# Starting three 64 KB-per-partition load buffers at a multiple of 256 bytes in SBUF, in a decode kernel that streams its KV cache

## The chip, the cores and the metric

The kernel runs on one core of a Trainium2 chip. The metric is the device time of one execution in microseconds (us).

The profile is a record of one execution. PE is the matmul engine, DVE is VectorE, ACT is ScalarE, POOL is GpSimd, SP is the engine that issues the transfers. The trace also holds a record of each DMA packet: start, duration, bytes, queue.

## The reference, cut to what matters

```python
B, Sq, D = 2, 1, 1024
H, Sk, Dh = 32, 16384, 128
# k_cache, v_cache: (B, H, Sk, Dh) bf16, 268 MB each
q = (x @ wq).reshape(B, Sq, H, Dh).transpose(0, 2, 1, 3)
scores = einsum("bhqd,bhkd->bhqk", q, k_cache) * Dh ** -0.5
o = einsum("bhqk,bhkd->bhqd", softmax(scores), v_cache)
a = o.transpose(0, 2, 1, 3).reshape(B, Sq, H * Dh) @ wo
b = ...   # layer norm, two small linear layers, an MLP 1024 -> 3584 -> 1024
out = g * a + (1 - g) * b          # g = sigmoid(sum(x * gate_w))
```

One query per head against 16,384 keys: each byte of the caches is read once and hardly used. With the weights that is 572.5 MB from HBM.

## The kernel before

Everything large passes through a ring of three buffers of 65,536 bytes a partition, which make up 192 KB of each partition of SBUF. A transfer of K or of V fills one buffer whole (128 partitions x 65,536 bytes, 8.39 MB). The pools are laid out in the order in which they are entered, so the buffers start where the small constants end:

```python
    const = ctx.enter_context(tc.tile_pool(name="const", bufs=1))
    big = ctx.enter_context(tc.tile_pool(name="big", bufs=NBIG))       # NBIG = 3
    tpool = ctx.enter_context(tc.tile_pool(name="tpool", bufs=2))
    # ... (cut)
    def big_tile(name):
        return big.tile([P, SLOT], BF16, tag="big", name=name)         # SLOT = 32768 elements

    def load_k(i):
        t = big_tile("Kn")
        nc.sync.dma_start(
            out=t[:].rearrange("p (j d) -> p j d", d=Dh), in_=cache_rows(A_k_cache, i)
        )
```

`cache_rows` gives each partition one run of 65,536 bytes of HBM, and its place in the buffer is one run too. Per K buffer, DVE makes 16 transposes into the tile T and PE 64 matmuls on S; per V buffer, PE makes 64 matmuls on O. A transfer is issued when the buffer three transfers back has been used up.

As built, the constants end at byte 20,640 of the partition. The three buffers start at 20,640, 86,176 and 151,712: each is 160 bytes past a multiple of 256.

Of the kernel before, what the change touches and what calls it, by code (L numbers as in the profile page):

```python
# [10 lines left out]
FP32 = mybir.dt.float32  # L11
BF16 = mybir.dt.bfloat16
# [11 lines left out]
def kernel(  # L24
# [16 lines left out]
    P = nc.NUM_PARTITIONS  # L41
# [4 lines left out]
    G = 2  # L46
# [10 lines left out]
    SLOT = NJ * Dh  # L57
    NBIG = 3

    const = ctx.enter_context(tc.tile_pool(name="const", bufs=1))  # L60
    big = ctx.enter_context(tc.tile_pool(name="big", bufs=NBIG))
    tpool = ctx.enter_context(tc.tile_pool(name="tpool", bufs=2))
    ppool = ctx.enter_context(tc.tile_pool(name="ppool", bufs=1))
    stat = ctx.enter_context(tc.tile_pool(name="stat", bufs=2))
# [86 lines left out]
        out=perm[:].rearrange("k (h a) -> k h a", a=4),  # L151
        in_=ident_f[:].rearrange("k (a h) -> k h a", a=4),
    )
    neg_half = const.tile([P, 1], FP32)
    nc.vector.memset(neg_half[:], -0.5)
    ones_f = const.tile([P, P], FP32)
    nc.vector.memset(ones_f[:], 1.0)

    hmask = const.tile([P, G], FP32)
    nc.vector.memset(hmask[:], 0.0)  # L160
    for a in range(G):
        nc.vector.memset(hmask[64 * a : 64 * a + 64, a : a + 1], 1.0)



    kill = const.tile([P, 1], FP32)
    kill4 = const.tile([P, 4], FP32)
    for a in range(4):
        c0 = 32 * a + (16 if a < 2 else 0)
# [22 lines left out]
            channel_multiplier=1,  # L192
        )

    own = const.tile([P, 8], BF16)
    nc.vector.memset(own[:], 0.0)
    for a in range(4):
        nc.vector.memset(own[32 * a : 32 * a + 32, 2 * a : 2 * a + 2], 1.0)
# [411 lines left out]
```

## Time and profile before

Time before: 1341.06 us, the median of three runs (1341.02 to 1341.31). The page of the kernel before, its span, its engines' busy shares and its two busiest DMA queues (packets, MB, share of 16 engines' time):

```profile
span 1339.3 us, 12650 instructions
PE 830.6 (62%) x5415; PEld 380.9 (28%) x5415; DVE 709.3 (53%) x863; ACT 45.6 (3%) x100; POOL 14.5 (1%) x45
...
q1 hardware_dynamic: 12664, 572.54, 99.1%
q8 instruction: 42, 0.69, 0.2%
```

No compute engine is near full, and the 16 DMA engines together are at work 99.1% of the span. The windows view says the same by stretch; its last columns are the granted matmul clock, the DMA share and GB/s:

```profile
20.00:400.00 380.00, 246.34 (x1698) 115.62 (x1699) 215.66 (x265) 12.08 (x28) 4.76 (x12) 0.83 1.00 431
400.00:800.00 400.00, 251.35 (x1603) 118.22 (x1602) 213.52 (x253) 13.89 (x31) 3.37 (x10) 0.79 1.00 432
800.00:1200.00 400.00, 251.68 (x1435) 109.36 (x1434) 228.56 (x259) 13.65 (x30) 3.38 (x10) 0.81 1.00 432
```

The list of DMA issues gives the median time from issue to landing. A K or V transfer moves 8.39 MB, which at 432 GB/s takes 19.4 us; 37.7 us to land means that it was issued while nearly a whole other transfer was still ahead of it. So the DMA engines never wait for an issue:

```profile
Kn<-in_A_k_cache_dram SPq DMA_DIRECT2D x32, 52.3
Vn<-in_A_v_cache_dram SPq DMA_DIRECT2D x31, 37.7
```

The main compute groups (busy us and mean ns | idle before):

```profile
L307 PE MATMUL S<-T,z 128*128 128x512 bf16 x2048 | 596.2, 424 | 326.2 <-DVE T L299 310.3
L299 DVE STREAM_TRANSPOSE T<-Kn 128x1024 f32<-128x1024 f32 x512 | 612.0, 1229 | 267.5 <-DMA Kn<-in_A_k_cache_dram 218.6
```

And two moments of the timeline (start us, length): the last matmuls on O, which waited for the last V transfer, and the cast of the result:

```profile
1298.44 3.63 PE L351 MATMUL O<-Vn,PT 128*32 128x512 bf16 x32 [4.90 <-DMA Vn<-in_A_v_cache_dram]
...
1336.04 0.42 DVE L575 CAST rows<-out_acc 128x256 bf16<-128x256 f32 x1 [31.21 <-PE out_acc L392]
```

The packet records, gathered by size (this is a count over the trace's records, not a view of the profile):

```
kernel before, main queue; ns
bytes     packets  minimum  median   mean
4096        256      159      159    161.0
8192        768      309      313    314.3
14336       512      535      538    539.9
57344       128     2116     2119   2129.1
65536      8192     2418     2420   2426.0     (1431 of 8192 at 2418; 68 over by more than 100 ns)
```

From 4096 to 65,536 bytes the minimum rises by 2259 ns for 61,440 bytes: 27.2 GB/s for one engine, 435 GB/s for sixteen. With 8.4 ns a packet on top, that gives the minima at both ends.

### The profile page before, as it was taken

The page shows a single profiled execution, that of the slowest core. Times are in us where ns is not written, and L with a number is a line of the kernel's source. Part 1 is how long each engine was busy: PE and PEld are TensorE (multiplying, and loading weights), DVE is VectorE, ACT ScalarE, POOL GpSimd, SP SyncE. Part 2 cuts the span into 40 slices and gives each one's busy share as a digit, 9 for nine tenths or more (in the row PEclk, how much of TensorE's full clock was granted, in tenths as well). Part 3 has the DMA queues.
Part 4 walks back from the last instruction along what each step waited for, and adds up shares of the span by engine and source line. Part 5 has one row for each costly group of instructions (what it writes and reads, how often), then busy time and mean ns, then how long its engine had stood idle before and what let it go on. Part 6 is the DMA issues. An engine that isn't in the chain of part 4 may idle for free.

```text
span 1339.3 us, 12650 instructions
## 1 busy us (share of the span) xinstructions
PE 830.6 (62%) x5415; PEld 380.9 (28%) x5415; DVE 709.3 (53%) x863; ACT 45.6 (3%) x100; POOL 14.5 (1%) x45
## 2 busy tenths in 40 slices
PE   2577655677657755555776555577655556765664
PEld 2233222433225322222332222233222223322231
DVE  0666565366651665545666544556655455665530
ACT  0000000000000000000000000000000000000000
POOL 0000000000000000000000000000000000000000
PEclk9988877688776877778887777888777788877775
DMA  9999999999999999999999999999999999999997
GB/s 408 435 437 434 435 423 437 424 439 433 433 431 430 436 436 433 427 429 427 437 437 435 433 433 424 435 435 431 435 431 433 435 437 425 435 427 429 434 422 291
DMA packets 12728, 573.34 MB, mean 428 GB/s; under 512 B 1784, under 2 KB 1792, under 8 KB 2560
## 3 DMA queue, kind: packets, MB, share of 16 engines
q1 hardware_dynamic: 12664, 572.54, 99.1%
q8 instruction: 42, 0.69, 0.2%
q14 instruction: 14, 0.11, 0.0%
q10 hardware_dynamic: 8, 0.00, 0.0%
HBM read 572.53 MB, written 0.00 MB: 427 GB/s over the span
## 4 chain that ended last, share of the span: by engine, by line
PE 27%; DVE 24%; DMA 19%; another core or an unknown queue 14%; issue 13%; ACT 3%; SPq 0%; ACTq 0%; POOL 0%
DVE T L299 20%; PE S L307 14%; DMA Kn<-in_A_k_cache_dram 13%; PE O L351 7%; DMA Vn<-in_A_v_cache_dram 3%; DMA wo<-in_A_wo_dram 3%; PE misc L212 2%; PE misc L361 2%; PE misc L486 2%; ACT Pr L335 1%; DVE PT L339 1%; ACT Os L359 1%; DVE mx L328 1%; DVE mdiag L321 1%
## 5 line engine op out<-in xcount | busy, mean ns | idle before, releaser
L307 PE MATMUL S<-T,z 128*128 128x512 bf16 x2048 | 596.2, 424 | 326.2 <-DVE T L299 310.3
L299 DVE STREAM_TRANSPOSE T<-Kn 128x1024 f32<-128x1024 f32 x512 | 612.0, 1229 | 267.5 <-DMA Kn<-in_A_k_cache_dram 218.6
L307 PEld LDWEIGHTS <-z 128*128 128x128 bf16 x2048 | 218.4, 107 | 698.3 <-issue 535.7
L351 PE MATMUL O<-Vn,PT 128*32 128x512 bf16 x2048 | 121.4, 390 | 4.9 <-DMA Vn<-in_A_v_cache_dram 4.9
L378 DVE SCALAR_TENSOR_TENSOR OT<-misc,g_bc,rinv 128x2 bf16<-128x2 f32 x32 | 7.0, 219 | 158.3 <-PE misc L361 158.3
L351 PEld LDWEIGHTS <-PT 128*32 128x32 bf16 x2048 | 74.1, 140 | 51.0 <-issue 22.0
L212 PE MATMUL misc<-rs,ones_f 128*128 128x2 f32 x64 | 17.8, 348 | 79.1 <-DVE rs L371 79.1
L359 ACT COPY Os<-O 128x512 f32<-128x512 f32 x32 | 18.8, 586 | 1070.2 <-PE O L351 1070.2
L361 PE MATMUL misc<-osel,Os 128*128 128x2 f32 x256 | 33.7, 254 | 22.2 <-ACT Os L359 22.2
L318 DVE TENSOR_REDUCE m<-S 128x1 f32<-128x512 f32 x32 | 22.1, 692 | 36.9 <-PE S L307 36.9
L361 PEld LDWEIGHTS misc<-osel,Os 128*128 128x128 f32 x256 | 31.0, 191 | 37.1 <-ACT Os L359 37.1
L212 PEld LDWEIGHTS misc<-rs,ones_f 128*128 128x128 f32 x64 | 16.0, 310 | 83.9 <-issue 81.2
L339 DVE STREAM_TRANSPOSE PT<-Pr 128x512 bf16<-128x512 bf16 x32 | 22.7, 711 | 28.7 <-ACT Pr L335 28.7
L335 ACT ACTIVATE Pr<-S,nb 128x512 bf16<-128x512 f32 x32 | 22.0, 687 | 125.3 <-DVE nb L330 122.3
L212 PE MATMUL misc<-mdiag,ones_f 128*128 128x128 f32 x64 | 15.6, 326 | 16.9 <-DVE mdiag L321 16.9
L486 PEld LDWEIGHTS <-wt 128*128 128x128 bf16 x352 | 22.3, 172 | 9.8 <-DMA wt<-in_B_w_dram 8.5
L328 DVE TENSOR_REDUCE mx<-misc 64x1 f32<-64x64 f32 x64 | 14.2, 222 | 18.9 <-PE misc L212 18.5
L275 POOL TENSOR_TENSOR z<-qsel,own 128x32 bf16<-128x32 bf16 x32 | 10.8, 337 | 1208.6 <-PE S L307 1177.3
L250 PE MATMUL misc<-xT,wt 128*128 128x2 bf16 x256 | 7.1, 165 | 23.3 <-DVE xT L245 20.7
L486 PE MATMUL misc<-xn2T,wt 128*128 128x2 bf16 x224 | 14.4, 202 | 8.3 <-DMA wt<-in_B_w_dram 8.3
L375 DVE RECIPROCAL rinv<-misc 128x2 f32<-128x2 f32 x32 | 5.5, 170 | 22.6 <-PE misc L212 22.6
L575 DVE CAST rows<-out_acc 128x256 bf16<-128x256 f32 x1 | 0.4, 424 | 31.2 <-PE out_acc L392 31.2
(78 smaller groups left out, 98.8 us busy)
## 6 DMA issues: line engine op xcount, KB each, us to landing
Vn<-in_A_v_cache_dram SPq DMA_DIRECT2D x2, 4096.0 KB, 47.1
wt<-in_B_w_dram SPq DMA_DIRECT2D x1, 7168.0 KB
w<-in_B_w_dram SPq DMA_DIRECT2D x4, 1792.0 KB, 33.0
wo<-in_A_wo_dram SPq DMA_DIRECT2D x6, 1024.0 KB, 34.7
wt<-in_B_w_dram SPq DMA_DIRECT2D x2, 2048.0 KB, 37.2
wo<-in_A_wo_dram SPq DMA_DIRECT2D x2, 512.0 KB, 18.9
wo<-in_A_wo_dram SPq DMA_DIRECT2D x4, 256.0 KB, 12.8
Kn<-in_A_k_cache_dram SPq DMA_DIRECT2D x32, 52.3
```

The costliest lines, as they stand in the source:

```text
L212: nc.tensor.matmul(ps[:], lhsT=ones_f[:], rhs=src, start=True, stop=True)
L299: nc.vector.transpose(out=T[:].rearrange("p w j s -> p j w s"), in_=Kw[:, m * CW : (m + 1) * CW].rearrange("p (j w e) -> p j w e", w=2, e=32),
L307: nc.tensor.matmul(S[:], lhsT=z[:, v, NM - 1 - m : NM - 1 - m + P], rhs=Tb[:, v // 2, :, v % 2], start=(m == 0 and v == 0), stop=(m == NM ...
L318: nc.vector.reduce_max(out=m[:], in_=S[:], axis=AX.X)
L321: nc.vector.tensor_scalar(out=mdiag[:], in0=ident_f[:], scalar1=m[:, 0:1], scalar2=None, op0=ALU.mult)
L328: nc.vector.reduce_max(out=mx[pa, :], in_=mall[pa, pa], axis=AX.X)
L335: nc.scalar.activation(out=Pr[:], in_=S[:], func=ACTF.Exp, bias=nb[:], scale=scale, accum_out=rs[:])
L339: nc.vector.transpose(out=PT[:], in_=Pr[:])
L351: nc.tensor.matmul(O[32 * g : 32 * g + 32, :], lhsT=PT[:, m : CJ * 32 : 16], rhs=V[:, j0 : j0 + 4, :], start=(m == 0), stop=(m == NM - 1),)
L359: nc.scalar.copy(out=Os[:].rearrange("p x d -> p (x d)"), in_=O[:])
L361: nc.tensor.matmul(oc[:], lhsT=Os[:, x, :], rhs=osel[:, x, :], start=(x == 0), stop=(x == 3))
L486: nc.tensor.matmul(ps[:, c, :], lhsT=w[:, r, :].rearrange("k (p c) -> k p c", c=C)[:, :, c], rhs=actT[:, r, :], start=(r == 0), stop=(r == ...
```

## The change

The intent is to start each buffer at a multiple of 256 bytes. The pool of buffers moves to the front. Only 256 bytes lie between byte 16,384, where the tiles begin as built, and the buffers: the language's own four constants (128 bytes) and four small tiles of this kernel (32 bytes each as allocated).

```diff
+    small = ctx.enter_context(tc.tile_pool(name="small", bufs=1))
+    big = ctx.enter_context(tc.tile_pool(name="big", bufs=NBIG))
     const = ctx.enter_context(tc.tile_pool(name="const", bufs=1))
-    big = ctx.enter_context(tc.tile_pool(name="big", bufs=NBIG))
@@
-    neg_half = const.tile([P, 1], FP32)
+    neg_half = small.tile([P, 1], FP32)
@@
-    hmask = const.tile([P, G], FP32)
+    hmask = small.tile([P, G], FP32)
@@
-    kill = const.tile([P, 1], FP32)
+    kill = small.tile([P, 1], FP32)
@@
-    own = const.tile([P, 8], BF16)
+    own = small.tile([P, 8], BF16)
```

As built, the buffers start at 16,640, 82,176 and 147,712, all multiples of 256. The tiles behind (T, Pr, PT, statistics) keep their addresses. The instructions and their order are the same on all five engines.

## The prediction

> **What bounds the kernel now.** The transfers. The page's queue list gives the main DMA queue 99.1% of the time of 16 engines; the windows view shows a DMA share of 1.00 and 431 to 432 GB/s from 20 to 1280 us. The matmul engine is 62% busy, VectorE 53%. The chain of waits names transposes and matmuls, but these only hand buffers back: a V load lands 37.7 us after its issue, about two transfers, so another one is always running and the DMA engines never run dry.
>
> By the trace's packets: 8192 of them carry 65,536 bytes each, minimum 2418 ns, median 2420, mean 2426. Minima of 159 ns at 4096 bytes and 2418 at 65,536 give 27.2 GB/s for one engine plus a constant of 8.4 ns a packet. Sixteen of these make 435.2 GB/s[...]. So: 572.5 MB at that slope 1315.6 us; about 680 data packets per engine x 8.4 ns 5.7 us; time over the minima 6 us; 1.8 us before the first packet; the rest is the tail.
>
> **What the change does.** Order and number of instructions stay the same on all engines; only addresses move. As built, the three buffers start 160 bytes past a multiple of 256 before, and at one after. T, Pr, PT and the statistics keep their addresses; constants swap places with the buffers, costed at nothing.
>
> [...] The whole constant would be 5.7 us. [...]
>
> Against it: [...] The 4-byte semaphore packets take 9 ns, and the first small loads' 16-byte packets 9 ns too[...]. So the constant may have nothing to do with alignment, and the gain be 0. [...]
>
> **Predicted.** 1338.8 us (before 1341.06), 8 in 10 between 1335.8 and 1341.8: in truth two places, near 1337 and near 1341. Faster by over 2%: 0.01; within 2%: 0.98; slower by over 2%: 0.01.
>
> **What would show it.** Right, if the minimum of the 65,536-byte packets falls from 2418 to about 2412 ns, and that of the 4096-byte ones from 159 to 153: the same nanoseconds at every size. Wrong, if the minima stay. Transposes (1229 ns) and matmuls on S (424 ns) should keep their means, apart from the clock. The tail after the last V transfer, from about 1298 us, should shrink by tenths at most.
>
> **What would make it wrong.** [...]

The sum: about 6 ns less in each of about 680 packets an engine came to 4.0 us, so near 1337, at somewhat less than an even chance, against a gain of 0, near 1341. The forecast of 1338.8 us, 2.3 under 1341.06, lies between these two. The trace has the 8.4 ns a packet (from the minima of 159 and 2418 ns); that 6 of them hang on the alignment was not shown. Cut with it are the reason given why a gain over 2% has no room, a doubt whether a write pays at all for its alignment, and a risk: if the time over the minima comes from misaligned writes that meet the engines' reads, aligned ones could save up to 4 us more, or lose as much.

## The result, and the profile after

The changed kernel takes 1337.38 us (median of 4 runs, 1337.28 to 1337.59), the kernel before 1341.18 us beside it (4 runs, 1341.02 to 1341.39): 3.8 us less. The ratio is 0.9972 with a 95% interval of 0.9954 to 0.9989. It is the mean time of one kernel's fast runs over that of the other's of the same rounds, so not quite the ratio of the medians.

The lines of the page after (line numbers are one higher than before):

```profile
span 1335.5 us, 12650 instructions
PE 830.0 (62%) x5415; PEld 381.4 (29%) x5415; DVE 709.2 (53%) x863; ACT 45.5 (3%) x100; POOL 14.3 (1%) x45
...
q1 hardware_dynamic: 12664, 572.54, 99.2%
```

The windows view after: the same DMA share, 1 GB/s more in each stretch.

```profile
20.00:400.00 380.00, 245.95 (x1702) 115.63 (x1703) 216.40 (x266) 12.07 (x28) 4.71 (x12) 0.83 1.00 432
400.00:800.00 400.00, 251.01 (x1605) 118.17 (x1604) 213.95 (x253) 13.88 (x31) 3.32 (x10) 0.79 1.00 433
800.00:1200.00 400.00, 253.82 (x1439) 109.99 (x1437) 228.87 (x259) 13.63 (x30) 3.31 (x10) 0.81 1.00 433
```

The issues and the compute groups after. Transfers land a little sooner; transposes and matmuls take what they took, so nothing came from the compute engines:

```profile
Kn<-in_A_k_cache_dram SPq DMA_DIRECT2D x32, 51.9
Vn<-in_A_v_cache_dram SPq DMA_DIRECT2D x31, 37.4
```

```profile
L308 PE MATMUL S<-T,z 128*128 128x512 bf16 x2048 | 594.0, 423 | 324.7 <-DVE T L300 309.7
L300 DVE STREAM_TRANSPOSE T<-Kn 128x1024 f32<-128x1024 f32 x512 | 611.8, 1229 | 264.1 <-DMA Kn<-in_A_k_cache_dram 215.8
```

The two moments of the timeline after:

```profile
1295.12 3.64 PE L352 MATMUL O<-Vn,PT 128*32 128x512 bf16 x32 [5.05 <-DMA Vn<-in_A_v_cache_dram]
...
1332.26 0.42 DVE L576 CAST rows<-out_acc 128x256 bf16<-128x256 f32 x1 [29.92 <-PE out_acc L393]
```

The last V data is used 3.3 us earlier (1298.44 to 1295.12) and the result is cast 3.8 us earlier (1336.04 to 1332.26). The gain was gathered evenly along the stream, and 0.5 us of it in the weight pieces at the end.

Even the packet records look alike at first, in the minimum and in the transfer rate. The difference is in how many packets reach the minimum:

```
65,536-byte packets       before    after
minimum, ns                 2418     2418   (one packet of after: 2415)
median, ns                  2420     2418
mean, ns                  2426.0   2422.8
at 2418 or less            17.5%    96.9%
over by 1 to 99 ns          6693      182
over by 100 ns and more       68       76
4096-byte packets: 159 at best in both; at 159: 161 of 256 before, 256 of 256 after
```

Below, "short excess" is the mean time over 2418 ns of the long packets, without those over by 100 ns and more. It is 3.38 ns before and 0.29 ns after. By transfer, in the order in which they ran, it goes like this (ns, the first 14 of the 64 transfers with such packets, and the last three):

```
before  1.0 6.3 1.9 1.2 2.2 1.8 2.7 2.6 3.4 3.4 3.9 3.4 3.3 3.2 ... 3.3 3.4 3.5
after   1.5 8.6 1.2 2.0 0.2 0.8 0.5 2.5 0.4 0.0 0.7 0.2 0.0 0.0 ... 0.0 0.0 0.0
```

Both begin alike. Then the kernel before settles at 3.5 ns and the kernel after at nothing.

The sum, in means over 16 engines: from the first data packet to the end of the last takes 1333.3 us before and 1329.7 after, 3.6 us less. Long packets give 1.7 us of that (1242.12 to 1240.46), shorter data packets 0.6 (84.20 to 83.60), instruction fetches on the other queues 0.4 (3.24 to 2.88), idle engines 1.0 (2.9 to 1.9, nearly all in the last 16 us). These are rounded and overlap a little at the edges. About half of the idle part has a visible source: the engines finish their shares of the last 14,336-byte pieces 3.0 us apart before (1312.05 to 1315.09) and 2.4 us apart after (1309.30 to 1311.66), so that the mean engine is done 2.1 us ahead of the slowest before and 1.6 us after.

### The profile page after: what moved, and what is told of

It reads as the page before. It is cut to its first block, busy times and chain, and to the rows that moved or that the text cites. A ratio compares the mean times of both kernels' runs of the same rounds, so it can differ in the third digit from the quotient of the medians.

```text
span 1335.5 us, 12650 instructions
## 1 busy us (share of the span) xinstructions
PE 830.0 (62%) x5415; PEld 381.4 (29%) x5415; DVE 709.2 (53%) x863; ACT 45.5 (3%) x100; POOL 14.3 (1%) x45
## 4 chain that ended last, share of the span: by engine, by line
PE 27%; DVE 24%; DMA 19%; another core or an unknown queue 14%; issue 13%; ACT 3%; SPq 0%; ACTq 0%; POOL 0%
DVE T L300 20%; PE S L308 14%; DMA Kn<-in_A_k_cache_dram 13%; PE O L352 7%; DMA Vn<-in_A_v_cache_dram 3%; DMA wo<-in_A_wo_dram 3%; PE misc L213 2%; PE misc L362 2%; PE misc L487 2%; ACT Pr L336 1%; DVE PT L340 1%; ACT Os L360 1%; DVE mx L329 1%; DVE mdiag L322 1%
## 5 line engine op out<-in xcount | busy, mean ns | idle before, releaser
L300 DVE STREAM_TRANSPOSE T<-Kn 128x1024 f32<-128x1024 f32 x512 | 611.8, 1229 | 264.1 <-DMA Kn<-in_A_k_cache_dram 215.8
```

The lines of the kernel that those rows point to most:

```text
L300: nc.vector.transpose(out=T[:].rearrange("p w j s -> p j w s"), in_=Kw[:, m * CW : (m + 1) * CW].rearrange("p (j w e) -> p j w e", w=2, e=32),
```

## The experiments

Twelve kernels were run. All keep T within 96 bytes of its old address, and T stays exactly in place in all but the last. Each is compared with the kernel before on the same chip. All passed the comparison with the reference, also those that compute a wrong attention: the comparison does not notice it (probably because the attention adds very little to the output; this was not looked into).

A column used in the tables is the pace: the mean time from one 8.39 MB transfer to the next, taken from the mean start of their packets, over the 50 such steps after the first dozen that have no weight load between them. It is 19.426 us before and 19.386 after. Times 68 (572.5 MB are 68 such transfers) the difference of 0.039 us makes 2.7 of the 3.8 us. A step between mean starts covers the second half of one transfer and the first half of the next; this matters in experiment 6.

### 1. Offset, or place of the constants?

The change does two things: it moves the start of the buffers to a multiple of 256, and it moves most constants, which all engines read, from in front of the buffers to behind them. Two kernels do one each. `off160` keeps the new order and pushes the buffers back to 160:

```diff
-    g_bc = const.tile([P, B], FP32)
-    omg_bc = const.tile([P, B], FP32)
+    g_bc = small.tile([P, B], FP32)
+    omg_bc = small.tile([P, B], FP32)
@@ the same for xn1T, hT, shT (32 bytes each)
```

> Pools in the order of the changed kernel (small constants, big buffers, other constants), but five 32-byte constants more in front, so that the buffers start 160 bytes past a multiple of 256, as in the kernel before; T keeps its address. Theory A (what counts is the offset of the buffers): 1341 us, and about 80% of the 65,536-byte packets over the minimum of 2418 ns again, by 3.5 ns on the mean. Theory B (what counts is that most constants, which all engines read, moved away from in front of the buffers): 1337.4 us, and over 95% of the long packets at 2418 ns.

`first0` keeps the old order and takes 160 bytes of constants away from in front:

```diff
     big = ctx.enter_context(tc.tile_pool(name="big", bufs=NBIG))
+    late = ctx.enter_context(tc.tile_pool(name="late", bufs=1))
@@
-    g_bc = const.tile([P, B], FP32)
+    g_bc = late.tile([P, B], FP32)
@@ the same for omg_bc, xn1T, hT, shT
```

> Pools in the order of the kernel before (constants in front of the buffers), but five 32-byte constants put behind them, so that the buffers start at a multiple of 256 (here also of 4096); T keeps its address. Theory A (offset): 1337.4 us, over 95% of the long packets at the minimum of 2418 ns. Theory B (place of the constants): 1341 us, 80% of them above it.

Measured:

```
kernel   offset mod 256   constants   us (median, 5 runs)   at 2418 ns   short excess   pace us
off160        160          behind          1341.15            18.0%        3.45 ns      19.426
first0          0          in front        1337.39            97.3%        0.21 ns      19.387
the kernel before beside them: 1341.16 us (9 runs)
```

Theory A, the offset, holds on both sides; the place of the constants is worth nothing. `first0` also lies at a multiple of 4096, and is no faster for it.

### 2. Which multiple?

The same edit with one, two or four tiles moved gives offsets of 32, 64 and 128.

> As the changed kernel, with two 32-byte constants more in front: buffers 64 bytes past a multiple of 256. Theory A1 (a write must start at a multiple of 256[...]): about 1341 us, most long packets above 2418 ns, by 3 to 4 ns on the mean. Theory A2 (only whole 64-byte units matter; 160 is a multiple of 32 but not of 64): 1337.4 us, over 95% of the packets at 2418 ns.

> As the changed kernel, with four 32-byte constants more in front: buffers 128 bytes past a multiple of 256. A1 (256): about 1341 us. A2 (64) or a unit of 128: 1337.4 us. A cost that grows with the offset up to half of 256 would show 128 as dear as or dearer than 160 and 64 at about half.

> As the changed kernel, with one 32-byte constant more in front: buffers 32 bytes past a multiple of 256, the least offset that the pools allow. All or nothing, as 64, 128 and 160 showed: 1341.2 us, 70 to 90% of the long packets above 2418 ns. If 32 bytes cost less than the others: between 1337.4 and 1341.

```
offset mod 256   us (median)   kernel before beside it   at 2418 ns   short excess   pace us
   0  (after)      1337.38            1341.18              96.9%        0.29 ns      19.386
  32               1342.08            1341.34               5.0%        4.49 ns      19.436
  64               1341.36            1341.16              11.5%        3.67 ns      19.428
 128               1341.19            1341.16              27.4%        3.47 ns      19.427
 160 (before)      1341.18              -                  17.5%        3.38 ns      19.426
```

Multiples of 64 and of 128 bring nothing (A2 falls). Of the offsets tried only 0 is free. The cost is not in proportion to the offset: 64, 128 and 160 cost 3.8 to 4.0 us over the changed kernel. The expectation "all or nothing" missed for 32, which costs 4.7 us over the changed kernel (4.5 if each is set against the kernel before on its own chip): it is 0.74 us over the kernel before on its chip (the others at most 0.2), with 95% of its packets over 2418 ns instead of the expected 70 to 90%. Offsets of 96, 192 and 224 were not tried.

### 3. Do the writes meet the engines' reads?

The prediction's own suspect was that misaligned writes meet the compute engines' reads of SBUF. `light160` and `light0` do a sixteenth of the work on each K and V buffer, at the old and at the new offset; the transfers are all there. Their outputs are wrong, which doesn't matter for the times.

```diff
-        for m in range(NM):          # transposes and matmuls on S
+        for m in range(1):
@@
-        for m in range(NM):          # matmuls on O
+        for m in range(1):
@@ start and stop flags to match
```

> Wrong result on purpose. The kernel before (buffers at 160) with a sixteenth of the work on each K and V buffer: one transpose of 16 and four matmuls of 64 on S, four of 64 on O; all transfers stay. Theory C (the time over the minimum comes from writes that meet the engines' reads and writes of SBUF): the mean short excess of the long packets falls from 3.5 ns to under 0.5 ns, and the time to about 1337 us. Theory D (it comes from the transfers among themselves): the excess stays at 3 to 4 ns and the time at about 1341 us less at most 1 us of the tail.

> Wrong result on purpose. The changed kernel with the same sixteenth of the work. C and D alike: about 1337 us, nearly all long packets at 2418 ns; it is the partner of the run before. If both light kernels take the same time, C holds; if they are 3 to 4 us apart, D.

The span, and the group of transposes, of the light kernel with offset 160:

```profile
span 1332.8 us, 4072 instructions
...
L299 DVE STREAM_TRANSPOSE T<-Kn 128x1024 f32<-128x1024 f32 x32 | 39.8, 1245 | 353.3 <-DMA Kn<-in_A_k_cache_dram 353.3
```

and of the light kernel with offset 0:

```profile
span 1329.6 us, 4072 instructions
...
L300 DVE STREAM_TRANSPOSE T<-Kn 128x1024 f32<-128x1024 f32 x32 | 39.8, 1245 | 352.0 <-DMA Kn<-in_A_k_cache_dram 352.0
```

512 transposes have become 32 and 612 us of them 39.8, and still the two kernels are 3.2 us apart: 1334.56 and 1331.39 us (5 runs each). At offset 160 the short excess is 3.48 ns, as with full work (3.38); at offset 0 it is 0.10. Theory C falls, D holds in the main: the excess in the packets is as large with a sixteenth of the compute. The totals are 6.7 us (offset 160) and 6.0 us (offset 0) lower than with full work, which D had not foreseen (it allowed 1 us). The 6.0 us are there without any misalignment, so they aren't the effect under study; the last section comes back to them. The other 0.6 us is the difference between 3.8 and 3.2 us; whether compute adds that much to the cost of the offset was not tested.

### 4. Source or destination?

The offset could count where a transfer reads, where it writes, or as a shift between the two. These two kernels read K and V from 160 bytes further on in HBM, once with the destination at 160 (same shift on both sides) and once at 0. The values are then wrong.

```diff
-        return cache[b, hg * G : (hg + 1) * G].rearrange("a s d -> (a s) d").rearrange(
-            "(p j) d -> p j d", p=P
-        )
+        e0 = (b * H + hg * G) * Sk * Dh + (80 if i < NT - 1 else 0)
+        return cache.rearrange("b h s d -> (b h s d)")[e0 : e0 + P * SLOT].rearrange(
+            "(p j d) -> p j d", p=P, d=Dh
+        )
```

> Wrong result on purpose. The kernel before (buffers at 160), and every K and V transfer but the last pair reads its 65,536 bytes a partition from 160 bytes further on in HBM, so that source and destination have the same offset to a multiple of 256. Theory R (what costs is the shift between source and destination): 1337.4 us, most long packets at 2418 ns. Theory W (what costs is where the write starts): 1341 us as before, excess 3.5 ns. [...]

> Wrong result on purpose. The changed kernel (buffers at a multiple of 256), reading K and V from 160 bytes further on in HBM. Theory R (shift between source and destination): 1341 us, excess 3.5 ns. Theory W (where the write starts): 1337.4 us, over 95% of the long packets at 2418 ns. [...]

```
kernel           source shifted by   destination mod 256   us (median)   at 2418 ns   short excess
src160_dst160          160                  160              1341.27        16.7%       3.39 ns
src160_dst0            160                    0              1337.45        97.3%       0.21 ns
the kernel before beside them: 1341.25 us
```

Theory W holds: where the write starts is what counts. Shifting the read by 160 bytes changes nothing, neither the minimum (2418 ns with the shift and without, but for single packets of 2415) nor the excess. (That the caches themselves start at a multiple of 256 in HBM is assumed; no run shows their addresses.)

### 5. One engine alone, or only in company?

`alone160` and `alone0` append eight loads of K rows into one buffer after the end of the kernel, each waiting for the one before, so that they meet neither compute nor other loads. (The scheduler put the first of them before the output, where it met the last weights. The second of each pair is read.)

```diff
+    pt = big_tile("probe")
+    for n in (17, 17, 34, 34, 68, 68, 128, 128):
+        nc.sync.dma_start(
+            out=pt[0:n, :].rearrange("p (j d) -> p j d", d=Dh), in_=cache_rows(A_k_cache, 0)[0:n]
+        )
```

> The kernel before with eight more loads into one buffer (at 160) after the end, each waiting for the one before it: 17, 17, 34, 34, 68, 68, 128, 128 partitions of 65,536 bytes, of which the second of each pair counts. If a DMA uses as many engines (up to 16) as divide its partitions, these run on 1, 2, 4 and 16 engines, and the engine count can be read from how many packets run at once. Theory D1 (engines get in each other's way[...]): alone, on 1 engine, every packet takes 2418 ns; the excess comes with 16. Theory D2[...]: an excess of 3 to 4 ns on the mean on 1 engine too.

> The changed kernel with the same eight loads (buffer at a multiple of 256), as partner. D1 and D2: 2418 ns for nearly every packet at every engine count, but for the first packets of a load, which start together.

(D1: the excess comes only with company. D2: each engine pays for its misaligned writes by itself.)

How many engines ran is read as the sum of the packets' times over the load's length; it comes near the 1, 2, 4 and 16 that the expectation supposed:

```
partitions  engines   short excess at offset 160   at offset 0    GB/s (160 / 0)
   17         1.0              0.00 ns               1.50 ns       26.4 / 26.5
   34         2.0              0.00                  0.75          53.1 / 52.8
   68         3.8       (see the last section)                     69.3 / 69.9
  128        15.5              1.23                  1.57         407.8 / 410.1
```

On one engine, at the costly offset, every packet but the first takes 2418 ns exactly. So an engine that runs by itself pays nothing for a misaligned write, in loads of 17 packets: D2 falls as far as these short loads go. But D1's second half was not met either: 16 engines in one isolated load show no more excess at 160 than at 0. The cost appeared only where all engines streamed for longer. That agrees with the series by transfer above, where both kernels begin alike and part after some five to ten transfers, that is 40 to 80 packets an engine. One engine alone was not tried for so long, so company and duration are not told apart here; experiment 6 speaks for company. `alone0` is not at 2418 ns for nearly every packet, as expected, but at 2420 for many; I have no reason for these 2 ns.

### 6. Does each buffer pay for itself?

Two theories: by P each packet pays for the offset of its own buffer, in the company of others; by L one misaligned buffer spoils all. Here the three buffers lie at 0, 32 and 64 past a multiple of 256:

```diff
-        return big.tile([P, SLOT], BF16, tag="big", name=name)
+        return big.tile([P, SLOT + 16], BF16, tag="big", name=name)[:, 0:SLOT]
```

> The changed kernel with 32 bytes between the buffers: the first starts at a multiple of 256, the second 32 bytes and the third 64 bytes past one (T moves by 96 bytes). Theory P[...]: a third of the long packets at 2418 ns, mean short excess a third of 0 + 4.6 + 3.8, so 2.8 ns; time 1337.4 + (0 + 4.7 + 4.0)/3 = 1340.3 us. Theory L[...]: under 25% of the packets at 2418 ns, excess 3.5 ns or more, 1341 us or more.

Measured: 1340.39 us (5 runs), beside 1341.21 for the kernel before; 56.8% of the long packets at 2418 ns, short excess 2.03 ns.

```
buffer, in the order of use            0        64        32
step to the next transfer, us        19.385   19.435    19.419
the same steps, changed kernel       19.377   19.398    19.383
more than there, us                   0.008    0.037     0.036
short excess, ns                      0.9       0.8       4.4
short excess, all three there, ns     0.01      3.77      4.63
(all after the first dozen transfers)
```

The time is the one that theory P gave (1340.3), but the bill by buffer is not P's. A step holds half of a transfer and half of the next, so each difference is half the sum of what its two transfers cost, and the three have to be solved for the buffers: my estimate from them is about 0.01 us a transfer for the buffer at 0, 0.01 for the one at 64 and 0.065 for the one at 32. P had nothing, 0.042 and 0.050 (the paces of experiment 2 over the changed kernel's). The packets say the same: the buffer at 64 is nearly free here, and the one at 32 pays in full. P's packets missed too (56.8% at the minimum, not a third). That its total came out is a coincidence of sizes. Theory L falls by its numbers (under 25% at the minimum, 1341 us or more).

The records show one thing more. After the first dozen transfers, 236 packets into the aligned buffer overlap in time (by more than 20 ns) with a packet that another engine writes into the buffer at 32: their short excess is 3.1 ns on the mean, against 0.6 ns for the 1799 that do not. For the buffer at 64 it is 2.8 ns (265 packets) against 0.5 (2024). In the changed kernel such packets at the edge of a transfer are not late (0.01 ns over all its later packets). So packets come late beside other engines' writes into the buffer at 32, also when their own buffer is aligned. Why the buffer at 64 costs 3.77 ns a packet when all three lie there and so little here is not known.

## Why the prediction was right or wrong

The time was right: 1338.8 predicted, 1337.38 measured, within the range of 1335.8 to 1341.8, and near the first of its "two places, near 1337 and near 1341". What bounds the kernel was right: with the same compute (1229 ns a transpose before and after) the time fell by what the transfers gained. The slope of 27.2 GB/s did not move (minima of 159 and 2418 ns in both kernels), and the gain was 0.28%, far from 2%; that the slope could not move was not shown.

The step that failed is the one that carried the number: about 6 of the 8.4 ns a packet as a cost of the alignment, 4.0 us in all. The prediction gave its own test, the minimum "falls from 2418 to about 2412 ns, and that of the 4096-byte ones from 159 to 153", and "Wrong, if the minima stay." They stayed at 2418 and 159. The 8.4 ns a packet are no cost of this misalignment; one engine alone at offset 160 also takes 2418 ns a packet. Nor does the cost grow with the offset: 32 cost more than 160 (1342.08 against 1341.18 us).

What happened stood in the prediction's last paragraph as a risk: the time over the minima (2426 against 2418) shrank, for which up to 4 us were allowed. That term, put at zero in the sum, is where the gain is: the share of long packets above the minimum went from 83% to 3%. But the reason given there, writes that meet the engines' reads, is wrong as well, for at least 3.2 of the 3.8 us: so far apart the two offsets still were with a sixteenth of the compute. And the mean excess that vanished is 3 ns, not the 8 between 2426 and 2418: more than half of those 8 are some 70 packets over by 100 ns and more, which stayed. That two wrong causes gave the right size is luck: the 4.0 us of the one happen to be near the 3.8 us measured.

The doubt whether a write pays at all had the wrong end: a shifted read costs nothing here (1341.27 against 1341.25 us), and the write is what counts (1337.45 us with its start at a multiple of 256). "The tail ... should shrink by tenths at most" was right: 0.5 of the 3.8 us came after the last V data was used.

What is shown: the offset of the destination to a multiple of 256 is the cause; the place of the constants and the source's offset are not, nor, for the most part, is the compute; a single engine does not pay in a load of 17 packets; and packets into an aligned buffer come late beside other engines' misaligned writes. The cost is no fixed price of a buffer's own offset, as the buffer at 64 in `mixed` shows. What stays open: in what way 16 engines delay each other by some nanoseconds a packet once they have streamed for several transfers, and why aligned writes escape it. No run here shows what becomes of a single misaligned write at the destination, nor why the buffer at 64 was nearly free in `mixed`.

## What to carry to other kernels

In a kernel whose DMA engines are busy all the time (99.1% of the span here), start the buffers of long loads at a multiple of 256 bytes in SBUF: it costs only the order of the pools and gave 0.28% here, while 64 or 128 gave nothing (1341.36 and 1341.19 us against 1341.16). Look up the built addresses, since a small tile added in front shifts the buffers: one of 32 bytes took the whole gain away again (1342.08 us). And when the records of a long stream pile up at a minimum, count what share of them reaches it: mean and minimum alone hid the difference between 17.5% and 96.9%.

## What else the runs showed

- The runs show no cost of a shifted read for long packets: with the source shifted by 160 bytes the minimum of the 65,536-byte packets stays 2418 ns, but for one of 2415, and the time is 1337.45 us. They show a cost of the write: 3.8 to 4.7 us of 1341 us in a full stream with all three buffers at any offset tried (32, 64, 128, 160), none in loads of 17 packets an engine on one or two engines.
- A multiple of 256 brought 0.28%, and a multiple of 4096 no more (1337.39 against 1337.38 us).
- A long packet has a constant of about 8.4 ns on top of 27.2 GB/s, at offset 160 as at 0 (by the minima of 159 and 2418 ns, the same in both kernels), of which neighbours on one engine share 4 ns (packets of 2418 ns that start 2414 ns apart).
- A load on few engines was far slower than their number says. With 68 partitions it ran on 3.8 engines at 69 to 70 GB/s, with packets over 2418 ns by 1126 to 1229 ns on the mean, while 34 partitions on 2 engines gave 53 GB/s at full rate. Why was not tested.
- What instruction fetches take from this kernel is shown in part. With 4072 recorded instructions instead of 12,650 the kernel was 6.0 us faster at offset 0 (1331.39 against 1337.38 us) with the same data moved. The instruction queue fell from 42 to 12 packets and the long packets over by 100 ns and more from 76 to 35. By the packet records the fetches' own time fell by 1.9 us an engine and those long delays by 1.0 us; where the other half of the 6 us comes from was not tested.
